# Two transposes of the exponentials ahead of q's maxima in VectorE's queue, with the order settled around them

## The chip, the cores and the metric

The kernel runs on one core of one Trainium2 chip. The metric is the time of one execution on the device in microseconds (us). The kernel before was run three times; the median is taken. One more execution was recorded by the hardware profiler, and all durations and start times below are from that one, counted from its first instruction. The engines are TensorE (PE, with its weight loads as PEld), VectorE (DVE), ScalarE (ACT), GpSimd (POOL) and SyncE (SP), which issues nearly all of the DMA.

## The reference

A transformer-like block with 2048 rows, width 512 and float32 data. Half A is a linear attention with 32 heads of 16 features; half B mixes rows by shifts and then runs an MLP of width 1376. Cut to what is computed:

```python
mod = (silu(c) @ w_mod)                      # six rows of 512: sa, ca, ga, sb, cb, gb
h = layernorm(x) * (1 + ca) + sa
q, k, v = split(h @ wqkv)                    # 32 heads of 16
pq, pk = q @ w_phi, k @ w_phi                # per head, 16x16
phi_q = concat(softmax(pq), softmax(-pq)); phi_k = concat(softmax(pk), softmax(-pk))
kv, z = phi_k^T v, sum over rows of phi_k
o = (phi_q kv) / (phi_q z + 1e-6)
x = x + ga * (o @ wo)
h = layernorm(x) * (1 + cb) + sb             # then half B on h
g = gelu(layernorm(h) @ w1); hs = shifted(g) @ w2; x1 = h + hs
x = x + gb * (x1 + gelu(layernorm(x1) @ w3) @ w4)
```

## The kernel before

Rows are handled in 16 tiles of 128, and mostly in 8 chunks of two tiles (256 rows). Every large product is made of three matmuls on high and low halves in fp32r, so each operand is split by a pair of operations: a copy to the high half on ScalarE (mostly), and a subtraction that gives the low half on VectorE or GpSimd (`hi_lo`, whose subtraction has line 418 on VectorE and 420 on GpSimd in the profile).

The program is a list of 2801 numbered operations, made in one run of the function `body`. Each operation has an engine, the tiles that it reads and writes, and for some of them another engine that could do it. The list is not issued in the order in which it is made: the constant `ORDER` is a permutation of the 2801 numbers, written out by hand. A letter behind a number (V, G or A) puts that operation on VectorE, GpSimd or ScalarE in place of its own engine. `emit` walks `ORDER`, so each engine's queue is the subsequence of `ORDER` that belongs to it, and every engine works through its queue strictly in that order. The constant `SLOT` says for each tile which buffer of its kind it gets. An operation waits by semaphores for the operations whose results it reads, and for the last readers of the buffer that it overwrites.

The first part (to about 145 us) makes k, v and q of all chunks. `q_feat` of tile t (group `q8` for tile 8 and so on) makes q's projection (12 matmuls with 512 columns, PE, `pp<-w,hh`), copies it to `qt` (ScalarE, for most tiles), takes the maximum and the minimum over the 16 features of each head (two reductions on VectorE, L442, `q<-qt` with 512 elements; these are q's maxima), subtracts them (GpSimd, `qe<-qt,q`), takes two exponentials (ScalarE, `qe<-qe`) and stores the result to DRAM.

The sums over k are then turned into two constants: `zbc` (group `z`) and `kvb` (group `kvb`). For `kvb` ScalarE copies the accumulated `kva`, TensorE spreads it by 8 small matmuls (`pp<-const,kvs`), and one VectorE operation masks it into SBUF (`const<-pp,const`, L418, number 682).

From about 145 us on, `phase_a(c)` works on chunk c. `q_phi(c)` loads the stored exponentials of two tiles into `e` (the loads rearrange blocks), sums them per head (`q<-e`, L442), multiplies them by `zbc` (`ez<-e,const`, groups `phi0`, `phi1` and so on) and sums these (`pz<-ez`, L442), then makes the weights of the two tiles in five small operations (group `den0` for the first chunk), scales both `e` by them (`e<-e,q`, GpSimd), and transposes each in blocks of 32 by 32 (`turn`, L762, `pT<-e`; groups `tr0` and `tr1` for the first two tiles). Then TensorE makes the numerators (`num0`: 64 small matmuls `pp<-pT,const`, which read `kvb` and `pT`), the output projection (`o0`: 24 matmuls `pp<-w,oT`), which VectorE adds to x with row sums (L437, `pp<-pp,xl`), then a layer norm (`rs<-mv` on GpSimd is its inverse root), a second one, transposes on TensorE (`pt<-const,n`), the split into `nT` (hi on ScalarE, lo on VectorE), and the first product of half B (`g0`, `pa<-nT,w`, 24 matmuls each half). While the first chunks go through this, the last eight tiles of q are still being made: q8 to q15 lie interleaved with `phi`, `den`, `tr`, `num` and `o` of chunks 0 to 2 in all queues.

From about 204 us on TensorE works through the rest of half A, the shifts and the MLP to the end.

VectorE's queue around the change, by numbers in `ORDER` (the engines' own work between them is left out):

```
708 706 (ez of tiles 1, 0)  709 707 (their sums)  460 459 (q8 max/min)  710-714 (den0)  796 798 (e sums 2, 3)
800 (phi2 sum)  467 (q9)  718 (pT, tile 1)  468 (q9)  590 (q12)  682 (kvb)  716 (pT, tile 0)  802 (phi3 sum)
524 (q10)  803 (den1)  589 (q12)  525 (q10)  722 (oT lo)  ...
```

Of the kernel before, what the change touches and what calls it, by code (L numbers as in the profile page):

```python
# [164 lines left out]
)  # L165
SLOT = {
    "pp": "510234426360573046405216574732325716511600313075732270653365216523706542035040435752736700267672"
          "4243153510404460571",
    "bd": "46",
    "w": "134625cd387165ad28cb09",  # L170
    "rk": "73958dgc",
# [1216 lines left out]
```

## Time and profile before

| what | value |
|---|---|
| runs | 554.64, 554.66, 555.55 us; median 554.66 us |
| profiled execution | 554.69 us; its span from first to last instruction 552.9 us |
| PE busy | 544.9 us (99%) in 4498 matmuls |
| DVE busy | 488.6 us (88%) in 903 instructions |
| ACT busy, POOL busy | 351.7 us (64%), 344.5 us (62%) |
| granted TensorE clock | 0.999 of full speed |
| DMA | 124.90 MB, mean 226 GB/s |

A row of the timeline gives the start in us, the duration in us, the engine, the line of the kernel, the operation, the tiles written and read, the size, and the count when several instructions of one kind follow each other; in brackets stands how long the engine had been idle before, and what released it. Matmuls are pipelined and their ends are modelled, so a row's end can lie a little behind the start of the next. A row of the windows gives, for one stretch of the span, the busy time of each engine and the granted clock.

### The profile page before, as it was taken

How to read it: one execution, taken by the hardware profiler on the slowest of the kernel's cores; microseconds unless marked ns; L12 is line 12 of the kernel's file. 1: busy time of each engine (PE TensorE's matmuls, PEld its weight loads, DVE VectorE, ACT ScalarE, POOL GpSimd, SP SyncE). 2: the span in 40 equal slices, each digit the busy share in tenths (PEclk: the TensorE clock that was granted, in tenths of full speed). 3: DMA queues.
4: the chain of work that ended last, by engine and by line, in shares of the span. 5: the costliest groups of instructions: out<-in, count | busy, mean ns of one | idle time of the engine just before them, and what ended most of it. 6: DMA issues, size and time to landing. Idle time of an engine off the chain costs nothing.

```text
span 552.9 us, 12370 instructions
## 1 busy us (share of the span) xinstructions
PE 544.9 (99%) x4498; PEld 488.1 (88%) x4498; DVE 488.6 (88%) x903; ACT 351.7 (64%) x828; POOL 344.5 (62%) x351
## 2 busy tenths in 40 slices
PE   8999999999989999999999999999999999999997
PEld 7888788878767788888889898999999999999996
DVE  3999999899999999999998878987888868896886
ACT  2899898834436788969888877866434543434540
POOL 2499985979599999978886545234150434254442
PEclk9999999999999999999999999999999999999999
DMA  8982544537736766869987878986689673872022
GB/s 323 392 277 89 175 170 137 176 112 248 205 118 226 249 195 206 275 235 319 292 275 270 242 257 301 339 356 231 284 248 347 245 284 97 264 286 80 25 92 95
DMA packets 63749, 124.90 MB, mean 226 GB/s; under 512 B 7140, under 2 KB 26852, under 8 KB 59592
## 3 DMA queue, kind: packets, MB, share of 16 engines
q1 hardware_dynamic: 63400, 124.04, 66.4%
q8 instruction: 35, 0.57, 0.4%
q14 instruction: 26, 0.21, 0.1%
q10 hardware_dynamic: 288, 0.07, 0.1%
HBM read 89.74 MB, written 34.35 MB: 224 GB/s over the span
## 4 chain that ended last, share of the span: by engine, by line
PE 86%; DVE 7%; POOL 3%; DMA 2%; issue 1%; ACT 0%; DVEq 0%; POOLq 0%
PE pp L471 36%; PE pa L471 27%; PE ac L471 20%; PE pt L480 2%; DVE pz L442 2%; DVE q L442 2%; DMA mod<-in_wmod 1%; PE kva L471 1%; POOL qe L420 1%; DVE pT L762 1%; POOL ez L420 1%; POOL e L420 1%; DVE ez L418 1%; DMA const<-in_c 1%; DVE pp L437 0%
## 5 line engine op out<-in xcount | busy, mean ns | idle before, releaser
L471 PE MATMUL pp<-w,hh 128*128 128x512 f32 x576 | 138.8, 397 | 0.0
L471 PEld LDWEIGHTS pp<-w,hh 128*128 128x128 f32 x576 | 106.7, 188 | 26.1 <-issue 1.6
L471 PE MATMUL pa<-bH,wq 128*128 128x256 f32 x840 | 106.7, 281 | 0.0
L471 PE MATMUL ac<-w,gg 128*128 128x256 f32 x840 | 106.6, 281 | 0.0
L471 PEld LDWEIGHTS ac<-w,gg 128*128 128x128 f32 x840 | 103.4, 189 | 1.1
L471 PEld LDWEIGHTS pa<-bH,wq 128*128 128x128 f32 x840 | 103.1, 189 | 0.9
L471 PE MATMUL pp<-w,sh 128*128 128x512 f32 x192 | 49.4, 399 | 0.0
L471 PE MATMUL pa<-nT,w 128*128 128x256 f32 x384 | 48.3, 282 | 0.8 <-DVE nT L418 0.7
L471 PEld LDWEIGHTS pa<-nT,w 128*128 128x128 f32 x384 | 46.8, 188 | 2.5 <-DVE nT L418 1.2
L471 PE MATMUL pp<-w,oT 128*128 128x512 f32 x192 | 47.4, 395 | 0.0
L471 PEld LDWEIGHTS pp<-w,oT 128*128 128x128 f32 x192 | 35.4, 188 | 8.1 <-DVE oT L418 0.7
L401 ACT ACTIVATE gg<-cu 128x256 fp32r<-128x256 f32 (+1 forms) x56 | 19.1, 359 | 35.1 <-PE ac L471 19.7
L471 PEld LDWEIGHTS pp<-w,sh 128*128 128x128 f32 x192 | 34.6, 188 | 7.5 <-issue 0.8
L588 POOL TENSOR_TENSOR rs<-mv,const 128x2 f32<-128x2 f32 x31 | 23.8, 769 | 25.3 <-ACT mv L595 23.7
L401 ACT ACTIVATE cu<-pa 128x512 f32<-128x512 f32 (+1 forms) x42 | 21.5, 519 | 27.6 <-PE pa L471 22.3
L420 POOL TENSOR_TENSOR gg<-cu,gg 128x128 fp32r<-128x128 f32 (+1 forms) x26 | 15.8, 615 | 33.2 <-ACT gg L401 13.9
L420 POOL TENSOR_TENSOR ez<-e,const 128x1024 f32<-128x1024 f32 x12 | 29.2, 2433 | 5.2 <-DMA dram<-qe 5.1
L401 ACT ACTIVATE gg<-sg 128x512 fp32r<-128x512 f32 x38 | 23.1, 624 | 14.0 <-POOL sg L420 6.0
L420 POOL TENSOR_TENSOR e<-e,q 128x1024 f32<-128x1024 f32 x15 | 28.8, 1938 | 0.4 <-DVE q L418 0.2
L418 DVE TENSOR_TENSOR gg<-cu,gg 128x256 fp32r<-128x256 f32 (+1 forms) x54 | 22.1, 416 | 7.6 <-PE ac L471 4.6
L418 DVE TENSOR_TENSOR gg<-sg,gg 128x512 fp32r<-128x512 f32 x36 | 26.0, 722 | 3.0 <-PE ac L471 1.5
L420 POOL TENSOR_TENSOR ke<-ke,k 128x1024 f32<-128x1024 f32 x14 | 27.2, 1952 | 1.2 <-DVE k L445 1.2
(214 smaller groups left out, 1211.5 us busy)
## 6 DMA issues: line engine op xcount, KB each, us to landing
wq<-dram SPq DMA_DIRECT2D x32, 1024.0 KB, 7.8
dram<-ws SPq DMA_DIRECT2D x35, 256.0 KB, 3.1
xl<-in_x SPq DMA_DIRECT2D x32, 256.0 KB, 4.1
dram<-qe SPq DMA_DIRECT2D x16, 512.0 KB, 3.7
e<-dram SPq DMA_DIRECT2D x64, 128.0 KB, 3.2
raw<-in_w SPq DMA_DIRECT2D x18, 256.0 KB, 3.7
mod<-in_wmod SPq DMA_DIRECT2D x16, 256.0 KB, 5.2
dram<-xl SPq DMA_DIRECT2D x16, 256.0 KB, 3.0
```

Source lines behind the costliest of these rows:

```text
L401: nc.scalar.activation(o(), i(), func, **kw)
L418: dve = ("DVE", 71 + 1.04 * o.n + 90 * (isps(a) and isps(b)), lambda: nc.vector.tensor_tensor(o(), a(), b(), op=op))
L420: pool = ("Pool", cost, lambda: nc.gpsimd.tensor_tensor(o(), a(), b(), op=op))
L442: plan.op("DVE", 65 + 1.04 * a.n + 110 * isps(o), lambda: nc.vector.tensor_reduce(o(), a(), axis=AX.X, op=op), [o], [a])
L471: nc.tensor.matmul(o(), a(), b(), start=s, stop=e, **kw)
L480: nc.tensor.transpose(o(), i(), ident())
L588: plan.op("Pool", 540 + 10 * m, lambda: nc.gpsimd.tensor_tensor(r(), v(), mhalf[:, :m](), op=OP.pow), [r], [v, mhalf])
L762: plan.op("DVE", 71 + 1.04 * o.n, lambda: nc.vector.transpose(o(), i()), [o], [i])
```

## The change

Only `ORDER` and `SLOT` differ. No operation is added, removed or altered. In VectorE's queue the two transposes of the first chunk (718 and 716) come ahead of maxima of q that stood before them: 718 ahead of 467 (q9), 716 ahead of 468 (q9) and 590 (q12). Around them the order is settled anew, which gives, in VectorE's queue of this stretch:

```
708 706 (ez of tiles 1, 0)  709 707 (their sums)  710-714 (den0)  460 459 (q8 max/min)  798 796 (e sums 3, 2)
800 (phi2 sum)  718 (pT, tile 1)  467 (q9)  716 (pT, tile 0)  468 (q9)  590 (q12)  802 (phi3 sum)  682 (kvb)
803 (den1)  589 (q12)  525 (q10)  804 (den1)  524 (q10)  722 (oT lo)  ...
```

So den0 moves ahead of q8's pair, and kvb (682) moves behind pT of tile 0, the rest of q9, q12 and the sum of phi3. In GpSimd's queue the scaling of tile 1 (717) moves ahead of q8's subtraction (461), q11's subtraction (534) moves ahead of the scaling of tile 3 (810), and a split of w3 (1005) ahead of the product of phi5 (909), which still stands ahead of the inverse root of o0 (741). In ScalarE's queue the copy for kvb (680) moves ahead of q9's copy and q8's exponentials, and the second normalised tile of n0 (757) ahead of the first (753). In SyncE's queue the store of q6 moves ahead of a load of x, and a load of the last weights (1481) behind the store of q8. TensorE's queue keeps the same sequence from 129 to 196 us but for one swap of v13 and v14.

Elsewhere in the list operations move by a few places (by 6 on average, counted in `ORDER`, at most 165), 117 of them get another engine (VectorE's queue has 858 operations in place of 871, GpSimd's 358 in place of 347, ScalarE's 736 in place of 734), and buffers are renamed. Seven of these 117 lie in the first 20 us, and all the others behind 290 us. The core of the diff:

```diff
 ORDER = (
...
-    "586 663 293 656 647 294 657 295 683 584 1481 381 684 797 603 685 605 672 383 652 457 708 1033 706 799G 458 "
-    "650 709 707 665 382 460 669G 384 459 903 710 465 862 711 461G 651 712 713 714 796 717G 462 798 654 466 587 "
-    "680 800 463 715G 464 467 718 801G 681 468 588 522 590 682 469G 716 802 905 719 523 720 907G 524 530 721 803 "
...
-    "906 593 594 733 904 687 810G 1001 1482 809 726 1004 1010 534G 734 727 689 735 688 736 812 728 536 694 909G "
...
+    "292 379 583 649 647 293 294 381 295 663 683 584 684 657 797 603 685 672 605 383 652 708 382 384 706 709 457 "
+    "799G 707 458 1033 650 903 669G 710 711 712 713 714 460 465 717G 651 459 798 461G 796 654 800 680 466 715G "
+    "462 718 587 463 464 467 801G 1481 716 681 588 468 522 590 469G 802 905 682 907G 803 589 719 523 720 525 530 "
...
+    "1001 906 593 1004 594 904 534G 733 687 809 726 1010 810G 734 689 727 735 688 536 736 1005G 812 728 694 811 "
+    "909G 737 738 739 729V 740 742 730 535 741 1012 744 813 690G 595 814 1007 743 745 816 537 910 985G 746 747 "
...
 SLOT = {
...
-    "ez": "4988322399990775",
+    "ez": "7388877733881994",
...
-    "pT": "3044399695373795",
+    "pT": "6279733584797084",
...
```

More of the change, by code (lines that the diff above doesn't have):

```diff
@@ L40 @@
 ORDER = (
[124 rows of a table removed]
[124 rows of a table added]
 )
 SLOT = {
[L167 to L171, printed above, removed]
-    "xl": "01lif20gi5bh89hdfh4a36c0kejafg2h50eh36ecj9hl0aac",
-    "st": "03b8g32eh379c16aej5837hgb7h96dj2b",
-    "mv": "14fa06bdj2bdg379c16c68i2h9ie7064a",
-    "rs": "26hc17fi148hj2bdg34j2a19ef1c4f78e",
-    "nm": "57ei9dj54a89cg056afei0548fhi02bd54bd03aiaeg0fj581cg539hi",
@@ L177 @@
-    "xn": "ab75aj6ejag7f54b",
-    "mod": "ekbk73e1dj930hf2ke",
-    "mod2": "1023",
-    "kva": "4",
-    "za": "7",
-    "hh": "0789abe0",
-    "pt": "71713064136760724740255030200105",
-    "raw": "948hcla7b2l2g59fd34940abi351",
-    "k1": "0110502430210140",
-    "ke": "4501639451823940",
-    "k2": "5343025543253140",
-    "vv": "3246ekjhkfh0170l",
-    "qe": "7692282134682731",
-    "q1": "3242123515032015",
-    "qt": "ajj9ib759209",
-    "acc": "clf1e",
-    "kvs": "1",
-    "pz": "1",
@@ L195 @@
-    "q2": "03105351",
-    "e": "5617956458034928",
-    "ez": "4988322399990775",
-    "q3": "1245243214024032",
-    "q5": "44423145",
-    "pT": "3044399695373795",
-    "oT": "4a4ea04b",
-    "nT": "b05444be",
-    "n": "l12l4aaf1h5kje7g",
-    "h": "7519l62c7i1lfkcd",
-    "gf": "21535500",
-    "sh": "92be2cb0",
-    "pa": "720435033552357536277143075740636220453477601263027041460272",
-    "wr": "80061",
-    "ws": "010ie23c3782d1hgibgibgfbd0id69267k7",
-    "gb": "8",
-    "tw": "08935",
@@ L212 @@
-    "bL": "47604149",
-    "nb": "dgdj5dhj4gg4jbjd",
-    "yt": "9fje7gehj940707c",
-    "bH": "23820419431994595628147378657521",
-    "tr": "e10a2k3haldgbhd0",
-    "wq": "e90c934e174e3174e7314e7134e14317e431",
-    "cu": "672egi14hdfl25b7c1364hg9ked6l14g9cd0jblf",
-    "gl": "big235l6",
-    "ac": "26311637061227465013415304762351",
-    "gg": "25789138572584716831287609283795063284107962583265103241806937415809261809713458",
-    "sg": "kf6fka6k0j0k94h3la253c4b4acl7276ki2k97e4",
-    "xb": "9had9ei0fj3haf15",
@@ L224 @@
-    "xc": "5le904k6jhi2fg2i",
-    "uu": "00k2i6ck",
+    "pp": "103254426360573024105642531076565142570060405012650736424542754275304217052353125077021243702025"
+          "7514373375161105643",
+    "bd": "34",
+    "w": "135624cd1803546c28ad79",
+    "rk": "62957dgc",
+    "xl": "01lkf81hf2c3e7faeg28bcia53digl83gf3hbda4h1b335a2",
+    "st": "02c8g25eh2afd3489j672ci3aaif4bh2a",
+    "mv": "13fa04abj5cbh2afd34d47e5ifg9c04f8",
+    "rs": "45hb38fd317ij5cbh21j580f9b3g1jc19",
+    "nm": "76ei9dj61c79ig0648e9g0617eig05ce61adj28e89h0bh67dg3567ie",
@@ new lines @@
+    "xn": "badc2j8ahk60l352",
+    "mod": "ei0k55ae907d1764j8",
+    "mod2": "1023",
+    "kva": "3",
+    "za": "0",
+    "hh": "0789abe7",
+    "pt": "71017321472114171713744334525754",
+    "raw": "3ibhbh069ajk10lf7bk1k7ie2c09",
+    "k1": "0154142304254534",
+    "ke": "4519637451823749",
+    "k2": "1303421130210101",
+    "vv": "dj54b943be4g74hl",
+    "qe": "7602282147569981",
+    "q1": "3202523540132140",
+    "qt": "j6cla90h4cae",
+    "acc": "glib8",
+    "kvs": "j",
+    "pz": "6",
@@ new lines @@
+    "q2": "03105451",
+    "e": "5610345046170836",
+    "ez": "7388877733881994",
+    "q3": "1245243213023042",
+    "q5": "55523450",
+    "pT": "6279733584797084",
+    "oT": "56be67ba",
+    "nT": "a74bbeab",
+    "n": "j9jk0k0f9h050cbf",
+    "h": "4h91j8c4a29jg5a8",
+    "gf": "82474611",
+    "sh": "92ae2da7",
+    "pa": "703114433732744470266315724172066332741566027321035460214535",
+    "wr": "89252",
+    "ws": "gkgi8jd7dfjeh4ge2l1l0e0lbi27d1lla5a",
+    "gb": "6",
+    "tw": "18406",
@@ new lines @@
+    "bL": "93512920",
+    "nb": "7lfdhf3hkffk1e18",
+    "yt": "1ghhfd431lk3j5e0",
+    "bH": "07781924496042747084970213281728",
+    "tr": "49li34c0d4h0f7b7",
+    "wq": "b97d91eb30eb130be310be301beb03b1e30b",
+    "cu": "dj4hfb7kg8id4jl97cg5gfe041h8i7lj02fi8bk7",
+    "gl": "0k0dbcja",
+    "ac": "63050516072335610247706274315620",
+    "gg": "86370698372387960859386014385616354827930168574689574638954160378521943501637285",
+    "sg": "i2i3d253a8a32f8a1d3jbcjlj3gi95g49agk051l",
+    "xb": "9gh1ei25ka3hecd9",
@@ L226 @@
+    "xc": "elee5g38b7k5g7g2",
+    "uu": "0g1d244k",
 }
```

239 rows, old and new, of the table ORDER are left out of this document.

## The prediction

> **What bounds the kernel now.** I read the busy times first, then the windows, to see which stage each engine fills.
>
> ```profile
> PE 544.9 (99%) x4498; PEld 488.1 (88%) x4498; DVE 488.6 (88%) x903; ACT 351.7 (64%) x828; POOL 344.5 (62%) x351
> ```
> ```profile
> 145.00:204.00 59.00, 56.48 (x486) 44.38 (x478) 58.05 (x90) 35.02 (x76) 55.88 (x35) 1.00 0.65 203
> 204.00:549.00 345.00, 345.00 (x2839) 326.49 (x2839) 298.45 (x614) 214.09 (x520) 180.71 (x227) 1.00 0.70 238
> ```
>
> TensorE looks like the only bound, but the windows split that. From 204 to 549 us it is busy 345.00 of 345.00 us, so whatever delay exists at 204 us is carried to the end. From 145 to 204 us, where the change sits, it loses 2.5 us, while VectorE is busy 58.05 and GpSimd 55.88 of 59.00 us: those two pace this stage. The timeline of TensorE shows where it waits.
>
> ```profile
> 157.71 3.04 PE L471 MATMUL pp<-w,hh 128*128 128x512 f32 x12
> 162.47 1.16 PE L471 MATMUL pp<-pT,const 64*32 64x128 f32 x64 [1.72 <-DVE pT L762]
> 163.56 3.03 PE L471 MATMUL pp<-w,hh 128*128 128x512 f32 x12
> 166.43 1.56 PE L471 MATMUL pp<-w,oT 128*128 128x512 f32 x6
> 167.83 2.94 PE L471 MATMUL pp<-w,hh 128*128 128x512 f32 x12
> 170.61 4.32 PE L471 MATMUL pp<-w,oT 128*128 128x512 f32 x18
> ...
> 188.76 0.28 PE L471 MATMUL pa<-nT,w 128*128 128x256 f32 x1
> 189.70 3.03 PE L471 MATMUL pa<-nT,w 128*128 128x256 f32 x23 [0.66 <-DVE nT L418]
> ```
>
> The longest wait, 1.72 us, is that of num0 for the second of the two transposes that are moved. The next is g0's for nT, 0.66 us behind its first matmul. Now VectorE and GpSimd in the same stretch.
>
> ```profile
> 144.80 4.56 DVE L418 TENSOR_TENSOR ez<-e,const 128x1024 f32<-128x1024 f32 x2 [0.23 <-ACT qe L401]
> 149.29 2.48 DVE L442 TENSOR_REDUCE pz<-ez 128x64 f32<-128x1024 f32 x2
> 151.67 1.27 DVE L442 TENSOR_REDUCE q<-qt 128x32 f32<-128x512 f32 x2
> 152.86 0.22 DVE L437 SCALAR_TENSOR_TENSOR pz<-q,pz 128x64 f32<-128x64 f32 x1
> ...
> 154.36 0.29 DVE L418 TENSOR_TENSOR q<-q,pz 128x128 f32<-128x128 f32 x1
> 154.56 2.34 DVE L442 TENSOR_REDUCE q<-e 128x64 f32<-128x1024 f32 x2
> 156.82 1.22 DVE L442 TENSOR_REDUCE pz<-ez 128x64 f32<-128x1024 f32 x1
> 157.94 0.68 DVE L442 TENSOR_REDUCE q<-qt 128x32 f32<-128x512 f32 x1
> 158.54 1.23 DVE L762 STREAM_TRANSPOSE pT<-e 128x1024 f32<-128x1024 f32 x1
> 159.69 1.24 DVE L442 TENSOR_REDUCE q<-qt 128x32 f32<-128x512 f32 x2
> 160.85 0.42 DVE L418 TENSOR_TENSOR const<-pp,const 128x256 f32<-128x256 f32 x1
> 161.18 1.24 DVE L762 STREAM_TRANSPOSE pT<-e 128x1024 f32<-128x1024 f32 x1
> 162.34 1.19 DVE L442 TENSOR_REDUCE pz<-ez 128x64 f32<-128x1024 f32 x1
> ```
> ```profile
> 145.46 2.82 POOL L420 TENSOR_TENSOR ez<-e,const 128x1024 f32<-128x1024 f32 x1 [5.13 <-DMA dram<-qe]
> ...
> 153.09 2.03 POOL L420 TENSOR_TENSOR qe<-qt,q 128x1024 f32<-128x1024 f32 x1 [2.50 <-DVE pz L437]
> 155.08 3.83 POOL L420 TENSOR_TENSOR e<-e,q 128x1024 f32<-128x1024 f32 x2
> 158.87 2.39 POOL L420 TENSOR_TENSOR ez<-e,const 128x1024 f32<-128x1024 f32 x1
> ...
> 175.53 2.40 POOL L420 TENSOR_TENSOR ez<-e,const 128x1024 f32<-128x1024 f32 x1
> 177.89 0.73 POOL L420 TENSOR_TENSOR ws<-wr,ws 128x256 fp32r<-128x256 f32 x1
> 178.59 0.69 POOL L588 TENSOR_TENSOR rs<-mv,const 128x2 f32<-128x2 f32 x1
> ```
>
> Each VectorE row starts where the last one ends, so a position in its queue is a time. The 160.85 row is kvb (682), the two transposes are pT of tile 1 and of tile 0.
>
> **The change part by part.** *VectorE up to num0.* I lay the new sequence on the old durations, from start to start. The sums of ez end at 149.29 + 2.48 = 151.77. den0 follows at once; its five operations take from 152.86 to 154.65, that is 1.8, so they end at 153.6 (before: 154.65). q8's pair (152.86 - 151.67 = 1.2) lasts to 154.7, the two e sums (2.26) to 157.0, the phi2 sum (1.12) to 158.1. pT of tile 1 starts there (before: 158.54). One reduction for q9 (0.6) and pT of tile 0 starts at 159.85 and ends at 161.1. Before it ended at 162.42. So far the change does what its name says: the transpose that num0 waited for is done 1.3 us earlier. Its input has to keep up: GpSimd scales tile 1 from 153.75 (0.15 behind den0, as 153.09 lies behind 152.94), then subtracts for q8 (1.99), then scales tile 0 until 159.6, just ahead of 159.85.
>
> *kvb.* num0 reads kvb as well, and kvb now stands behind pT of tile 0, the other q9 reduction, q12's (1.16 together) and the phi3 sum (1.1). It starts at 163.3 and ends at 163.7; before it ended at 161.27, 1.15 ahead of the transpose. So num0 starts at about 163.8 in place of 162.47: TensorE's q10 ended at 160.75, and its wait grows from 1.72 to 3.0 us. The wait goes from pT to kvb, and **1.3 us are lost at num0** where 1.3 were to be won. The bounds are the transpose alone (161.15, a gain of 1.3) and kvb (163.8); I take kvb, because the matmuls name the tile and nothing lies between. Queued behind num0 on TensorE are q11, o0, q14 in fixed order, and all shift.
>
> *What that costs further on.* TensorE arrives late in a stage that VectorE and GpSimd pace, so the loss counts only where they wait for it.
>
> ```profile
> 175.22 0.69 DVE L437 SCALAR_TENSOR_TENSOR pp<-pp,xl 128x512 f32<-128x512 f32 x1
> ...
> 179.31 0.75 DVE L437 SCALAR_TENSOR_TENSOR h<-pp,rs,const 128x512 f32<-128x512 f32 x1
> ```
>
> Between num0 and this point VectorE has the same work as before in a slightly different order, and every operand is there in time, with one exception: the second addition of o0 started at 175.22, and its matmuls ended at 170.61 + 4.32 = 174.93. The slack was 0.29. With TensorE 1.3 later they end at 176.25, so VectorE, which would be there at some 175.6, waits about 0.7, and the addition comes 1.0 later than before. The layer norm behind it needs the inverse root on GpSimd. There GpSimd too is later: its chain began at 153.75 in place of 153.09, and the phi5 product (175.53) now goes into the buffer of the third transpose, which num1's first half must have read; that half follows num0 by 174.93 - 162.47 = 12.4 on TensorE, so it ends at 163.8 + 12.4 + 0.6 = 176.8. The product then runs from about 176.95 to 179.35 and the inverse root from 179.4 to 180.1, against 178.59 to 179.28. So the 179.31 row moves to 180.15: **0.8 us late**. The two causes run side by side and aren't added. From here to nT and g0 (189.70), and on to g1 at about 204, VectorE and GpSimd have nothing to give (58.05 and 55.88 of 59.00 us), so I carry 0.8 to 204 us and, by the full row behind it, to the end. g0's wait of 0.66 takes up what TensorE is late beyond 0.8. Bounds of this term: 0, if VectorE and GpSimd make up their lateness on operations that wait a little now, and 1.3, if all of num0's loss goes through; 0.8 is what both chains give.
>
> *One collision that stays.* The row of 144.80 holds two products of 1024 elements in 4.56 us, while the sums of the same size take 1.24 each; GpSimd's product, 2.82 long where its like takes 2.39, began at 145.46 in the midst. One VectorE product has waited for GpSimd, by 4.56 - 2 x 1.2 = 2.2 us. The Trainium skill (SBUF — State Buffer, section Who interferes with whom) says that a VectorE instruction with two SBUF inputs and a GpSimd instruction that reads SBUF exclude each other, whoever issues first, and that one with a single SBUF input never contends; this trace agrees, since the transpose of 158.54 ran beside GpSimd's 158.87 in its usual 1.23. The three products stand in the same order after the change, and GpSimd's was released by the store of q5, which is as early or earlier now. If it comes first of the three, the sum of the three is the same. Cost 0; lower bound -2.2, if it came behind both of VectorE's.
>
> *ScalarE, SyncE and the swap in n0.* ScalarE is busy 35.02 of 59.00 us and covers its reordering; the swap of the two normalised tiles makes TensorE's transposes about 0.3 later, which g0's wait of 0.66 covers. The moved loads and stores here (q6's store, a load of last weights behind q8's store) lie tens of us ahead of their readers but for e of tile 5, which is loaded once q8's store has landed, at about 162 as before. Cost 0; without these covers up to 0.3.
>
> *The rest of the order.* Up to 145 us TensorE's sequence differs by exchanges of neighbours, and its inputs are the same. Behind 204 us VectorE has 298.45, GpSimd 180.71 and ScalarE 214.09 of 345.00 us, so the 110 operations that change engines are covered by idle time, one by one. I take 0, with bounds of 0 (nothing is left to win in a row of 345.00) and +1.0, about one exposed operation of GpSimd's size.
>
> **Sum.** 554.69 (the profiled execution, 1.8 us around its span of 552.9) + 0.8 = **555.5 us**. That execution lies 0.03 above the median of 554.66, which I neglect.
>
> **The rivals.**
> *The gain is returned (554.7).* If kvb weren't what num0 waits for, or VectorE absorbed its lateness, num0's 1.3 either way would end at g0, whose lo half of nT stands at the same place in a full queue: the wait moves from num0 to g0, and nothing changes. For it: VectorE at 98% of the stage. Against it: the 0.29 slack at 175.22 and GpSimd's later start.
> *The collision flips (553.3).* GpSimd's product begins at 145.46, and VectorE's second one would have started at 145.95. If q5's store releases GpSimd more than 0.5 us later than before, VectorE runs both products in 2.4 and is 2.2 earlier throughout the stage: 554.69 - 2.2 + 0.8. Against it: in ScalarE's queue q5's exponentials stand no later.
> *More waits behind 204 us (556.5).* The settled order has many new neighbours, and one exposed wait of 1 us adds in full, because TensorE is the bound there.
> *The clock falls (558.5).* If a wait of 3.0 us at num0 let the granted clock drop for the next 12 matmuls, their 3.03 would double and the wait at the o0 addition would grow by 3.0. The row has 1.00 after a wait of 1.72; no run here shows 3.0. The Trainium skill (TensorE: Matmul & The Clock Gate, section What's actually happening) puts the fall behind one idle window of about 3.4 us, which 3.0 doesn't fill; its summary names gaps over some 3 us.
>
> **How the numbers follow.** 0.2% of 554.66 is 1.1 us, about what this measurement can tell from no change: under 553.55 is faster, over 555.77 slower. Forecast 0.50 (555.0 to 556.0; I put 0.36 of it below 555.77 and 0.14 above), gain returned 0.20, collision flips or some other gain 0.12, more waits 0.14, clock 0.04. Faster 0.12, same 0.36 + 0.20 = 0.56, slower 0.14 + 0.14 + 0.04 = 0.32. The range leaves out the faster case, the clock and the top of more waits: 554.2 to 556.7.
>
> **What would show it.** Right: num0's row has an idle time near 3 us that ends on the masking of kvb (L418), not on L762; pT of tile 0 ends near 161.1; the second addition of o0 starts near 176.3 behind an idle VectorE; g1 starts 0.8 later. Wrong: num0 earlier than 162.47; GpSimd's product behind both of VectorE's at 145 us; a TensorE wait behind 204 us.

## The result

The changed kernel took 558.52 us (median), the kernel before beside it 554.90 us. The median counts a disturbed run of 1115.41 us; ratios and intervals leave such runs out here and below, and the other six lie between 556.97 and 559.50 us, with a median of 558.16. The ratio is 1.0059, with a 95% interval of 1.0045 to 1.0073: slower by 3.3 us, where 0.8 had been forecast. The profiled execution took 559.5 us, with a span of 557.4 us and a granted clock of 0.997. By the clock of the whole run, three took 557.79, 558.89 and 559.50 us at 0.997, and three 556.97, 557.58 and 558.52 us at 1.000: 1.0 us apart on average, though the two groups overlap.

### The profile page after: what moved, and what is told of

Same layout as the page of the kernel before. It is cut to its first block, busy times and chain, and to the rows that moved or that the text cites. A ratio compares the mean times of both kernels' runs of the same rounds, so it can differ in the third digit from the quotient of the medians.

```text
span 557.4 us, 12336 instructions
## 1 busy us (share of the span) xinstructions
PE 548.2 (98%) x4498; PEld 489.8 (88%) x4498; DVE 485.3 (87%) x890; ACT 353.7 (63%) x830; POOL 352.0 (63%) x362
## 4 chain that ended last, share of the span: by engine, by line
PE 65%; DVE 8%; POOL 1%; issue 1%; DMA 1%; ACT 0%; DVEq 0%
PE pa L471 27%; PE ac L471 20%; PE pp L471 17%; DVE q L442 2%; DVE pz L442 1%; PE pt L480 1%; DVE ez L418 1%; POOL e L420 1%; DVE pT L762 1%; DMA dram<-qe 1%; POOL ez L420 0%; DVE ke L418 0%; DVE qe L418 0%; DVE k L442 0%; DVE nT L418 0%
## 5 line engine op out<-in xcount | busy, mean ns | idle before, releaser
L471 PE MATMUL pp<-w,hh 128*128 128x512 f32 x576 | 140.6, 401 | 0.0
L471 PEld LDWEIGHTS pp<-w,hh 128*128 128x128 f32 x576 | 107.8, 190 | 27.1 <-issue 1.6
L471 PE MATMUL ac<-w,gg 128*128 128x256 f32 x840 | 106.9, 281 | 0.0
L471 PE MATMUL pa<-bH,wq 128*128 128x256 f32 x840 | 106.8, 282 | 0.0
L471 PEld LDWEIGHTS ac<-w,gg 128*128 128x128 f32 x840 | 103.8, 188 | 1.3
L471 PEld LDWEIGHTS pa<-bH,wq 128*128 128x128 f32 x840 | 103.2, 189 | 0.6
L471 PE MATMUL pp<-w,sh 128*128 128x512 f32 x192 | 49.5, 399 | 0.4 <-DVE nT L418 0.4
L471 PEld LDWEIGHTS pa<-nT,w 128*128 128x128 f32 x384 | 46.9, 188 | 2.4 <-DVE nT L418 1.0
L471 PE MATMUL pa<-nT,w 128*128 128x256 f32 x384 | 48.4, 282 | 0.5 <-DVE nT L418 0.3
L471 PE MATMUL pp<-w,oT 128*128 128x512 f32 x192 | 47.4, 396 | 0.0
L471 PEld LDWEIGHTS pp<-w,oT 128*128 128x128 f32 x192 | 35.5, 188 | 8.1 <-DVE oT L418 0.3
L471 PEld LDWEIGHTS pp<-w,sh 128*128 128x128 f32 x192 | 34.6, 188 | 8.2 <-issue 1.2
L588 POOL TENSOR_TENSOR rs<-mv,const 128x2 f32<-128x2 f32 x31 | 22.2, 715 | 18.9 <-ACT mv L595 15.6
L420 POOL TENSOR_TENSOR sg<-cu 128x128 f32<-128x128 f32 x23 | 14.3, 626 | 29.4 <-ACT cu L401 11.4
L418 DVE TENSOR_TENSOR gg<-sg,gg 128x512 fp32r<-128x512 f32 x37 | 27.9, 755 | 5.2 <-ACT gg L401 3.6
L418 DVE TENSOR_TENSOR gg<-cu,gg 128x256 fp32r<-128x256 f32 (+1 forms) x54 | 21.1, 403 | 9.5 <-PE ac L471 4.2
L420 POOL TENSOR_TENSOR gg<-cu,gg 128x128 fp32r<-128x128 f32 (+1 forms) x26 | 17.7, 688 | 17.9 <-ACT gg L401 5.7
```

The lines of the kernel that those rows point to most:

```text
L418: dve = ("DVE", 71 + 1.04 * o.n + 90 * (isps(a) and isps(b)), lambda: nc.vector.tensor_tensor(o(), a(), b(), op=op))
L420: pool = ("Pool", cost, lambda: nc.gpsimd.tensor_tensor(o(), a(), b(), op=op))
L471: nc.tensor.matmul(o(), a(), b(), start=s, stop=e, **kw)
L588: plan.op("Pool", 540 + 10 * m, lambda: nc.gpsimd.tensor_tensor(r(), v(), mhalf[:, :m](), op=OP.pow), [r], [v, mhalf])
```

## The profile after

The busy times of the page, and windows of the stage and of what is behind it. A window's columns are its length, then PE, PEld, DVE, ACT and POOL busy, the granted clock, DMA share and GB/s.

```profile
PE 548.2 (98%) x4498; PEld 489.8 (88%) x4498; DVE 485.3 (87%) x890; ACT 353.7 (63%) x830; POOL 352.0 (63%) x362
```
```profile
160.00:164.00 4.00, 1.72 (x8) 1.06 (x6) 4.00 (x7) 0.60 (x1) 4.00 (x2) 1.00 0.72 218
164.00:168.00 4.00, 3.87 (x71) 3.05 (x72) 4.00 (x9) 2.12 (x4) 4.00 (x3) 0.71 0.66 185
168.00:172.00 4.00, 4.00 (x17) 3.22 (x16) 2.11 (x6) 2.08 (x5) 3.09 (x3) 0.87 0.46 179
172.00:180.00 8.00, 8.00 (x64) 6.13 (x63) 7.57 (x12) 3.86 (x11) 7.10 (x5) 1.00 0.60 229
...
207.00:553.00 346.00, 345.57 (x2836) 326.55 (x2836) 294.89 (x602) 214.54 (x518) 188.18 (x239) 1.00 0.69 237
```

PE's busy time grew by 3.3 us for the same 4498 matmuls, which a wait can't do: some matmuls became longer. The windows show where about half of it lies. The clock column is below 1.00 from 164 to 172 us and in no other of them, and from 168 to 172 us VectorE, which paces this stage, is idle for 1.9 of 4.00 us. In the kernel before, the clock is 1.00 there (the first row below). Narrower windows of the changed kernel show that the clock was at half, for some 3.4 us, and that the fall began 1.5 us behind the start of num0:

```profile
164.00:168.00 4.00, 4.00 (x19) 3.26 (x18) 3.90 (x9) 2.61 (x6) 4.00 (x3) 1.00 0.93 280
```
```profile
164.10:165.60 1.50, 1.47 (x66) 1.23 (x67) 1.50 (x5) 0.27 (x1) 1.50 (x2) 1.00 0.78 237
165.70:169.00 3.30, 3.30 (x10) 2.51 (x9) 2.96 (x5) 1.75 (x4) 3.30 (x3) 0.50 0.76 237
169.10:172.00 2.90, 2.90 (x14) 2.33 (x14) 1.45 (x4) 2.08 (x5) 1.99 (x2) 1.00 0.22 87
```

The timeline of TensorE names the matmuls:

```profile
158.65 3.07 PE L471 MATMUL pp<-w,hh 128*128 128x512 f32 x12
164.13 1.16 PE L471 MATMUL pp<-pT,const 64*32 64x128 f32 x64 [2.41 <-DVE const L418]
165.22 4.61 PE L471 MATMUL pp<-w,hh 128*128 128x512 f32 x12
...
173.85 4.36 PE L471 MATMUL pp<-w,oT 128*128 128x512 f32 x18
...
323.06 0.94 PE L471 MATMUL pp<-w,sh 128*128 128x512 f32 x3 [0.43 <-DVE nT L418]
```

Read downwards: q10 starts 0.94 later than before (157.71). num0 waits 2.41 instead of 1.72, and the wait ends on kvb's mask (L418), no longer on the transpose (L762). Then q11's 12 matmuls take 4.61 instead of 3.03. The 18 of o0 start 3.24 later (170.61 before). The last row is a wait behind 206 us that the kernel before did not have. VectorE's and GpSimd's timelines, from the two products at 145 us on:

```profile
145.23 4.57 DVE L418 TENSOR_TENSOR ez<-e,const 128x1024 f32<-128x1024 f32 x2
...
160.23 1.23 DVE L762 STREAM_TRANSPOSE pT<-e 128x1024 f32<-128x1024 f32 x1
163.67 0.41 DVE L418 TENSOR_TENSOR const<-pp,const 128x256 f32<-128x256 f32 x1
178.25 0.70 DVE L437 SCALAR_TENSOR_TENSOR pp<-pp,xl 128x512 f32<-128x512 f32 x1 [0.43 <-PE pp L471]
```
```profile
178.96 2.41 POOL L420 TENSOR_TENSOR ez<-e,const 128x1024 f32<-128x1024 f32 x1 [0.90 <-PE pp L471]
181.32 0.70 POOL L588 TENSOR_TENSOR rs<-mv,const 128x2 f32<-128x2 f32 x1
```

The transpose of tile 0 ends at 161.46 (162.42 before), so it is early, and kvb ends at 164.08 (161.27 before). The second addition of o0 waits for TensorE (178.25 against 175.22), and GpSimd's phi5 product waits for num1, as the prediction had it from the changed buffer. VectorE's first product starts 0.43 later than before (145.23 against 144.80), so of TensorE's 0.94 not all has reached the engine that paces the stage. Three places thus show a loss: the start (0.94 at q10), num0 with the slow matmuls behind it, and the order behind 206 us. T1, T2 and T3 below name them as the main cause: T1 the wait at num0 and the clock behind it, T2 the start, T3 the rest.

## The experiments

In the kernels below, a line of the source is often one lower than in the two kernels above (L470 for L471); the operations are the same. Times are medians; each group of kernels has its own runs of the kernel before beside it, given as "before". Where two orders are joined, the first keeps its order up to the cut and the second goes on behind it; such a kernel also has a `SLOT` of its own, so buffers change with the order. The kernels with single moves keep `SLOT`.

### Start, middle and rest by themselves

```diff
 ORDER  (e1_start)
-before: words up to operation 104 (about 20 us)
+changed: words up to operation 104
 before: all others
 ORDER  (e2_middle)
-before: words from there up to operation 858 (about 206 us)
+changed: the same stretch
 ORDER  (e3_rest)
-before: words behind operation 858
+changed: words behind operation 858
```

> The new order up to about 20 us, the old one behind it. T1 (the wait that kvb's mask brings to num0, and the fall of TensorE's clock behind it, make the loss): nothing but the shift of the start, TensorE 0.5 us later from 10 to 20 us and to the end, 555.4 against 554.9 of the kernel before; wait at num0 1.7, q11's 12 matmuls 3.05. T2 (the start is where it is lost, and its shift grows): 556.5 or more. T3 (the rest behind 206 us): as T1.

> The new order from about 20 to 206 us alone (both transposes ahead, kvb's mask behind), the old one before and behind it. T1: wait at num0 2.4 to 3.0 that ends on kvb's mask (L418), the second addition of o0 late; 555.9 in runs where the clock holds and 557.5 where it falls, with q11's 12 matmuls at 4.6 instead of 3.05. T2 and T3: no more than 555.3.

> The old order up to about 206 us, the new one behind it. T1: 554.9 to 555.3. T3 (new neighbours behind 206 us cost a wait that nothing hides): 556.0 to 556.5, with a wait of 0.4 at 321 us that ends on nT (VectorE, L418) and TensorE 1 us later at the end than at 206 us.

Measured, against 554.78 us for before: the start alone 555.94 us, ratio 1.0018 (1.0007 to 1.0029); the middle alone 556.38 us, 1.0025 (1.0016 to 1.0034); the rest alone 556.13 us, 1.0024 (1.0013 to 1.0035). Each of them costs 1 us or more by the ratio, so no theory has it all (the start alone lies between what T1 and T2 expected): 1.0 + 1.4 + 1.3 = 3.7 us, of 3.3 measured for the whole. The wait of 0.4 at 321 us that T3 expected in the rest alone did not come.

The middle tells most. Its 12 runs fall in two groups with nothing between them: 555.49 to 555.89 us at clocks of 0.998 to 1.000 (six runs), 556.86 to 557.21 us at 0.995 to 0.997 (six runs). The gap between the groups' middles is 1.3 us, and the lower group is 0.9 us above before. The profiled run is of the upper group; its timeline of TensorE and its windows show the same fall as the changed kernel:

```profile
158.24 3.06 PE L470 MATMUL pp<-w,hh 128*128 128x512 f32 x12
163.72 1.16 PE L470 MATMUL pp<-pT,const 64*32 64x128 f32 x64 [2.42 <-DVE const L417]
164.81 4.62 PE L470 MATMUL pp<-w,hh 128*128 128x512 f32 x12
```
```profile
164.00:168.00 4.00, 4.00 (x72) 3.12 (x52) 3.97 (x8) 2.12 (x4) 4.00 (x2) 0.61 0.73 205
168.00:172.00 4.00, 4.00 (x18) 3.24 (x17) 2.13 (x5) 2.48 (x6) 3.05 (x3) 0.96 0.32 128
```

### kvb's mask put back ahead, and put behind by itself

In VectorE's queue, by numbers (718 and 716 are the transposes, 682 is kvb's mask):

```diff
 e4_after_kvb_early (from the changed kernel)
-718 467 716 468 590 802 682 803
+718 467 682 716 468 590 802 803
 e5_before_kvb_late (from the kernel before)
-467 718 468 590 682 716 802 524
+467 718 468 590 716 802 682 524
```

> The changed kernel with kvb's mask put back ahead of the transpose of tile 0, so that only the transposes are early. T1: kvb ends by about 161.5 and pT of tile 0 at about 161.9, the wait at num0 falls from 2.4 to 0.5 or less, the clock holds (q11's 12 matmuls 3.05), o0 2 us earlier; 556.0 to 557.0 against 558.5. T2 and T3: the wait goes, the time stays within 0.6 of 558.5, since start and rest are unchanged.

> The kernel before with one move in VectorE's queue: kvb's mask from ahead of the transpose of tile 0 to behind phi3's sum; the transposes stay. T1 (the late mask stretches the wait at num0, and behind a wait of 2.4 us and more TensorE's clock falls in part of the runs): wait at num0 2.6 to 3.0 that ends on the mask, granted clock under 0.9 in the 4 us behind it, q11's 12 matmuls at 4.6; runs in two groups 1.3 apart, about 555.9 and 557.2. Rival (the wait is taken up behind num0, the clock fall belongs to other edits): 554.9 to 555.3, q11 at 3.05.

With the mask early the changed kernel took 557.09 us, just above the range of T1, ratio 1.0036 (1.0024 to 1.0048) to before; all five runs had a clock of 0.999 or 1.000. Against the changed kernel (ratio 1.0059) this is 1.3 us less. The wait at num0 is gone, q11 takes its 3.06 again, and part of what num0 wins is waited for at the next step, o0, which needs VectorE's low half of oT:

```profile
161.29 1.16 PE L470 MATMUL pp<-pT,const 64*32 64x128 f32 x64
162.38 3.06 PE L470 MATMUL pp<-w,hh 128*128 128x512 f32 x12
165.28 0.62 PE L470 MATMUL pp<-w,oT 128*128 128x512 f32 x2
166.42 1.20 PE L470 MATMUL pp<-w,oT 128*128 128x512 f32 x4 [0.52 <-DVE oT L417]
```

With only the mask late, the kernel before took 556.89 us against 554.86, ratio 1.0039 (1.0025 to 1.0054), and all five runs had a clock of 0.996 or 0.997. One operation of 0.4 us, two places further back, costs 2.0 us. The two groups of runs that had been expected are one, the lower clock. The wait is longer than in the changed kernel, and the clock in the window lower:

```profile
163.63 1.16 PE L470 MATMUL pp<-pT,const 64*32 64x128 f32 x64 [2.81 <-DVE const L417]
164.72 4.57 PE L470 MATMUL pp<-w,hh 128*128 128x512 f32 x12
```
```profile
164.00:168.00 4.00, 4.00 (x64) 3.12 (x45) 3.42 (x7) 2.12 (x4) 3.50 (x2) 0.58 0.71 215
```

So the mask's place makes the wait and the fall, without the early transposes and without the rest of the order. The rival, that the wait is taken up behind num0, falls.

### The same wait with TensorE kept at work

```diff
 def phase_a(c):
...
+            if c == 0 and j == 0:
+                fill = ps[0].re("p k c -> p (k c)", (2 * CH,))
+                items = [(fill, wo[0][:, 0, :P], wo[0][:, 0, :], True, True) for _ in range(7)] + items
             marks["num", c] = mms(items, ps, [kvb, pT[j]], hold=[oT], tiles=8)
```

> The changed kernel with TensorE kept at work in the idle time ahead of num0: 7 more matmuls of 128x512 into num0's own PSUM buffer, which num0 overwrites; kvb's mask stays late. T1 (the idle time lets the clock fall): the wait shrinks from 2.4 to 0.7 or less, num0 still starts when the mask is done, q11's 12 matmuls are back at 3.05 and the granted clock at 1.00, no run with a lower mean clock; 557.5 against a median of 558.5. Rival (the clock falls for another reason): runs still fall into two groups, the slower ones with q11 at 4.6; median 558.5.

Measured: 557.13 us (556.97 to 558.02), ratio 1.0044 (1.0030 to 1.0057), and the clock at 1.000 in all five runs, where three of the changed kernel's six had 0.997. By the ratios the changed kernel became 0.8 us faster with seven matmuls more, but the two intervals overlap; the clock and q11's matmuls are the surer sign. The timeline:

```profile
159.55 3.07 PE L471 MATMUL pp<-w,hh 128*128 128x512 f32 x12
162.46 1.78 PE L471 MATMUL pp<-w 128*128 128x512 f32 x7
165.04 1.16 PE L471 MATMUL pp<-pT,const 64*32 64x128 f32 x64 [0.80 <-DVE const L418]
166.12 3.06 PE L471 MATMUL pp<-w,hh 128*128 128x512 f32 x12
```

num0 still waits for the mask, but only 0.80, and q11 takes 3.06. The idle time of TensorE, not the mask's lateness as such and not the amount of work, is what the clock follows here.

This kernel also shows the path behind a late mask while the clock holds. VectorE's rows:

```profile
146.13 1.23 DVE L418 TENSOR_TENSOR ez<-e,const 128x1024 f32<-128x1024 f32 x1
...
177.60 0.70 DVE L437 SCALAR_TENSOR_TENSOR pp<-pp,xl 128x512 f32<-128x512 f32 x1 [0.43 <-PE pp L471]
181.41 0.75 DVE L437 SCALAR_TENSOR_TENSOR h<-pp,rs,const 128x512 f32<-128x512 f32 x1
```

Counted from VectorE's first product at 145 us (144.80 before), num0 starts 1.24 later than before, the second addition of o0 1.05 and the row of h 0.77. The prediction had 1.3, 1.0 and 0.8.

Counted over all kernels, by num0's wait in the kernel's profile: 0 of 62 runs had a mean clock below 0.998 where the wait was at most 0.8 us (seven kernels); 14 of 165 at 1.7 us (the kernel before with 102 of these, and six kernels that keep its middle); 9 of 18 at 2.4 us; 5 of 5 at 2.8 us.

### Only the two transposes early

```diff
 e6_before_two_turns (from the kernel before)
-467 718 468 590 682 716 802
+718 467 682 716 468 590 802
```

> The kernel before with only the two transposes early: pT of tile 1 ahead of the first, kvb's mask and pT of tile 0 ahead of the second maximum of q9. T1: kvb ends near 160.7 and pT of tile 0 near 161.9, the wait at num0 falls from 1.7 to about 1.2 or less, the clock holds, and what num0 wins is given back at the second half of num0's copies and at g0, VectorE having the same work: 554.5 to 555.2, no difference from 554.9. Rival (num0's earlier start goes through): 554.0 or less.

The mask (682) moves forward with them, and stays ahead of the transpose of tile 0. Measured: 555.31 us against 554.86, ratio 1.0009 (1.0000 to 1.0018). num0 starts 1.45 us earlier (161.02 in place of 162.47; 0.27 of it is an earlier q10 in this execution), and all of it is lost on the way. The waits of TensorE in that kernel:

```profile
PE pp L470 <- DVE oT L417: 1.4, 2, 1.3
...
PE pa L470 <- DVE nT L417: 0.7, 1, 0.7
PE pp L470 <- DVE pT L761: 0.5, 1, 0.5
```

num0's wait fell from 1.7 to 0.5, and one of 1.3 for oT stands in its place, at 182.82. VectorE has the same work up to there.

### VectorE's collision at 145 us taken away

```diff
 e9_before_ez_apart (from the kernel before; VectorE, then GpSimd)
-708 706 709 707 460 459 710
+708 709 706 460 459 707 710
-799 669 862 461 717
+799 862 461 669 717
 e13_ez_and_turns: the same, and
-467 718 468 590 682 716 802
+718 467 682 716 468 590 802
```

> The kernel before with the products of phi0 and phi2 kept apart at 145 us: VectorE runs phi1's product, its sum, then phi0's product, so that GpSimd's product of phi2 does not meet it; the product for w7 goes behind q8's on GpSimd. If VectorE is what bounds 145 to 207 us, the product of phi0 takes 1.2 to 1.7 instead of 3.42, den0 starts 0.7 to 1.3 earlier, num0 0.7 earlier, and the time is 554.0 to 554.4. Rival (GpSimd or g0's inputs take it back): 554.7 to 555.0.

> The kernel before with both products kept apart at 145 us, as in the run before, and the two transposes and kvb's mask early. If VectorE's work up to nT is the bound, the transposes add nothing here either: 553.7 to 554.3, the wait at num0 gone, waits at o0 and g0 in its place. If num0 now counts: 553.3 or less.

Measured: 553.87 us against 554.86, ratio 0.9978 (0.9969 to 0.9987); with the transposes early as well 554.29 us against 554.97, 0.9985 (0.9977 to 0.9994). The first is a version that beats both kernels, by 1.0 us over the one before. VectorE's timeline shows phi0's product at 2.17 instead of the 3.4 that it had as the second in the row of 4.56, and den0 at 152.06 instead of 152.86:

```profile
145.14 1.22 DVE L417 TENSOR_TENSOR ez<-e,const 128x1024 f32<-128x1024 f32 x1 [0.23 <-ACT qe L400]
146.40 1.23 DVE L441 TENSOR_REDUCE pz<-ez 128x64 f32<-128x1024 f32 x1
147.54 2.17 DVE L417 TENSOR_TENSOR ez<-e,const 128x1024 f32<-128x1024 f32 x1
...
152.06 0.23 DVE L436 SCALAR_TENSOR_TENSOR pz<-q,pz 128x64 f32<-128x64 f32 x1
```

VectorE 0.8 earlier is worth 1.0 us at the end; num0 1.45 earlier without VectorE is worth nothing. With both (the second kernel) the transposes still add nothing.

### The start's loads and engines, and where the rest loses

```diff
 e10_start_loads (from the kernel before; SyncE)
-35 52 2 42 50 54 56 237 23 31 19 88 27
+52 35 2 42 50 54 56 23 31 19 88 237 27
 e11_start_engines: ORDER of e1_start, with these two moves of SyncE undone
 e12_late_rest: changed order behind about 330 us only
 e14_206_to_330: changed order from about 206 to 330 us only
```

> The kernel before with only the two moves of the start in SyncE's queue: the second part of the modulation's weights ahead of the first rows of x, and the rows xl5 behind four loads of the weights rk. T1 (the start's loss of 1.0 lies in the order of the loads): 555.5 to 556.2, TensorE's waits for the modulation's weights 0.2 to 0.5 longer. T2 (it lies in the operations that change engines): 554.7 to 555.1.

> The new start up to about 20 us with the loads in the old order, the old order behind it: operations change engines and neighbours alone. T1 (loads): 554.7 to 555.2. T2 (engines and neighbours): 555.5 to 556.2, and runs as far apart as with the whole new start (554.6 to 557.3).

> The old order up to about 330 us, the new one from there. If the loss of 1.2 of the rest lies in the waits at g6 and at 321 us: 554.9 to 555.2. If it is spread over the matmuls of the last 220 us: 555.5 to 555.9, TensorE's matmuls pa<-bH,wq of 128x256 at 97.3 or more in all from 330 to 550 us against 97.0, with no wait of its own.

> The new order from about 206 to 330 us alone, the old one before and behind it. The new order behind 206 us cost 1.2, the one behind 330 us nothing. If the loss is made between 206 and 330 us by waits there: 555.8 to 556.2, TensorE 0.8 or more later at 330 us. If it needs both parts: 554.9 to 555.2.

(In the first two of these texts T1 and T2 stand for the start's loads and for its changes of engine.) Measured, against 554.97 us: the loads alone 555.39 us, 1.0008 (0.9999 to 1.0017); the other moves of the start alone 555.61 us, 1.0009 (1.0000 to 1.0018); the order behind 330 us alone 554.95 us, 0.9999 (0.9990 to 1.0008). The order from 206 to 330 us alone, against 555.03: 555.31 us, 1.0006 (0.9998 to 1.0015). The start's two halves share its loss about evenly, and both intervals reach down to 1. The profile of the loads alone has a wait of 0.4 for the weights rk that neither whole kernel has, so that half is not a clean part. A part of the start's loss was made by the cut itself: with the changed start up to 20 us TensorE waits at 29 us for rows that VectorE normalises, which neither whole kernel does (the start alone, then the start without its loads):

```profile
29.25 0.98 PE L479 MATMUL pt<-const,xn 128*128 128x128 f32 x7 [0.56 <-DVE xn L409]
```
```profile
29.62 0.99 PE L479 MATMUL pt<-const,xn 128*128 128x128 f32 x7 [0.66 <-DVE xn L409]
```

The rest's 1.3 us is in neither of its parts: 0.3 and 0.0 by themselves. In the first of these two, the profile has a wait of 0.7 for gf at 325.69; in the rest as a whole TensorE's waits show none behind 206 us, but the matmuls themselves are a little longer. In the window from 330 to 550 us the 840 matmuls of `ac<-w,gg` are busy for 106.9 us in the whole rest and 106.8 in the part behind 330 us, the 768 of `pa<-bH,wq` for 97.3 and 96.9. Before has 106.6 and 97.0. In the whole rest that is 0.6 of the 1.3 us, spread over 1608 matmuls, though most of it in the first group is there in the part behind 330 us too, which costs nothing. Clearer is how long the products `ac<-w,gg` last from the first to the last, in the whole rest and in the part behind 330 us:

```profile
L470 PE MATMUL ac<-w,gg x840: 274/281/312, 351.8 to 550.0; 128*128 128x256 f32 x168
```
```profile
L470 PE MATMUL ac<-w,gg x840: 274/281/320, 351.6 to 549.0; 128*128 128x256 f32 x168
```

The two kernels have the same order there, yet the first takes 0.8 us more, without a wait. So this order does not lose the time by itself; it loses it behind the changed order from 206 to 330 us, or with other buffers. What lengthens the matmuls stays open.

### New up to 140 us, or from there

```diff
 ORDER  (e15_to_140)
-before: words up to operation 646 (about 140 us)
+changed: words up to operation 646
 ORDER  (e16_from_140): the reverse
```

> The new order up to about 140 us, the old one behind it, so that the two orders no longer meet at 20 us, where a wait of 0.6 to 0.7 for xn at 28 us belonged to neither kernel alone. If the start's loss is real: 555.5 to 556.0, TensorE 0.5 to 1.0 later at 146 us. If it was that wait: 554.9 to 555.3.

> The old order up to about 140 us, the new one behind it: the reverse of the run beside it. T1 with additive parts: the changed kernel without its start, 557.3 to 558.0, in two groups 1.3 apart by the clock behind num0. If the start's loss is not real: 558.3 or more.

Measured: 553.78 us against 555.03 for the first, ratio 0.9976 (0.9966 to 0.9987), and 555.75 us, 1.0014 (1.0005 to 1.0024), for its reverse. Both expectations missed. The first is faster than before, because the joint moved GpSimd's product: VectorE's two products come first, and GpSimd waits for them. VectorE's and GpSimd's timelines:

```profile
145.18 2.36 DVE L417 TENSOR_TENSOR ez<-e,const 128x1024 f32<-128x1024 f32 x2 [0.24 <-ACT qe L400]
...
151.04 0.22 DVE L436 SCALAR_TENSOR_TENSOR pz<-q,pz 128x64 f32<-128x64 f32 x1
```
```profile
146.37 3.45 POOL L419 TENSOR_TENSOR ez<-e,const 128x1024 f32<-128x1024 f32 x1 [5.86 <-DMA dram<-qe]
```

GpSimd's release came 0.9 us later than in the kernel before (145.46), the pair takes 2.36 instead of 4.56, and den0 starts 1.8 earlier. The reverse meets a wait of 1.5 us for vv at 145 us, in the joint, that neither kernel has, and its VectorE products are free of GpSimd too; so it cannot be read as the changed kernel without its start. What the start costs can be read from where q10 begins on TensorE. With the changed start it was 158.65 (the changed kernel), 158.09 (mask early), 159.55 (filled) and 158.13 (new up to 140 us), on average 158.6; in the nine profiles with the old start that have no wait of a cut's own 157.44 to 158.24, on average 157.84. That is about 0.8 us, with a scatter as large as itself from run to run. VectorE paces the stage, and its first product at 145 us starts at 145.30 and at 144.88 on average in the same two groups: about 0.4 us of the start reach it, with a scatter of the same size.

## Why the prediction was wrong

**Right: what num0 waits for.** The wait goes from pT to kvb (the 164.13 row names L418), the transpose comes 1.0 earlier (1.3 forecast), and GpSimd's phi5 product waits for num1. Moving the mask alone makes the wait and the fall of the clock, putting it back takes both away.

**Right: the sum of the path when the clock holds.** "0.8 us late" against 0.77 at the same row in the filled kernel, and 0.9 at the end in the middle alone, lower group.

**Mis-sized: the wait itself.** kvb ended at 164.08 instead of 163.7, but TensorE was 0.94 late already, so it waited 2.41 and not 3.0. This is a sign that the start was not free, where the prediction took 0 up to 145 us: 0.4 by VectorE's first product, and 1.0 (0.4 to 1.6) in the start alone, of which a wait of 0.56 belongs to the cut.

**Failed: the clock rival's condition.** It stood at 0.04, since 3.0 us was held to be too short a wait. With a wait of 2.4 us the clock was lower in half of the runs, with 2.81 us in all five. Its place was right (q11), its price was half of what was put: 4.61 against 3.03, 1.6 at the place and 1.3 at the end. All 12 matmuls at half clock would have taken 6.1, but the clock was at half for only some 3.4 us, which costs 1.7. The rival's 558.5 meets the measured median by chance: it lacks the start and the rest, and its price is too high.

**Failed: "The rest of the order", 0 with an upper bound of 1.0.** The order behind 206 us cost 1.3 (0.7 to 1.9). The argument was that idle time on the other engines covers 110 operations one by one. For waits this held nearly: the changed kernel has one of 0.43 at 323 us, and the rest alone none. What the step left out is that matmuls can become longer without a wait. The bounds of the term lay on one side of its value: with TensorE at 345.00 of 345.00 us a new order had little to win and something to lose. TensorE's own sequence is also another one behind 206 us, which the term did not weigh. Which operations do it was not found, and the cause stays open.

Put together: 0.4 from the start (1.0 with the wait of its cut), 0.9 at num0, 1.3 of clock in half of the runs, which is 0.7 on average, and 1.3 from the rest: 3.3 (3.9) against 3.3 measured. That this meets is in part luck, since the parts come from separate runs with intervals of about 0.6 each way.

**Right: the collision.** In the changed kernel it stayed, as forecast (4.57 for the two products). It does flip where GpSimd is released 0.9 later, at the place and by the condition given for the rival. VectorE then gains 1.8 to 2.2, of which 1.2 reach the end: num0's wait, 1.72, all but vanishes, and the rest is TensorE's own work. The Trainium skill (SBUF — State Buffer, section Who interferes with whom) says that whoever issues first holds the shared read path; the trace agrees in both orders, VectorE's product 3.42 when GpSimd came first, GpSimd's 3.45 when VectorE did. The prediction's "never contends" for one SBUF input is wider than that section of the Trainium skill, which excepts VectorE's two-port modes; this case shows it only for transposes (1.23) and sums (1.24).

**"The gain is returned"** was the wrong reading for this change but the right one for its title: the two transposes, with the mask still ahead, gave 1.45 at num0 and nothing at the end.

## What to carry to other kernels

Before moving an operation, list everything behind which its consumer's other operands now stand: here the late operand was a mask of 0.4 us, a few places back, and it cost more than the two moves in the title could win. Where the bounding engine is full, put the bounds of a resettled order on the side of loss: here it was 0.0 and 0.3 us for the two parts of the rest and 1.3 for both. Price a lone wait of TensorE of 2.4 us or more with the slower matmuls behind it.

What shortened this stage was time taken off the engine that paces it. Taking two colliding products apart was worth 1.0 us, starting TensorE 1.45 earlier nothing.

## What the hardware showed that was not expected

The mean clock of the run was below 0.998 in 9 of 18 runs of kernels with one idle time of TensorE of 2.4 us, in 5 of 5 with 2.8 us, in 14 of 165 with 1.7 us, and in none of 62 with 0.8 us or less. Where the fall lies is seen only in the profiled runs, of which three have one behind num0 (waits of 2.41, 2.42 and 2.81). The windows of the changed kernel have 0.50 from 165.7 to 169.0 us and 1.00 on both sides. Half clock for some 3.4 us lowers the mean over 557 us by 0.003, about the distance of the low runs from 1.000. In none of the three did the fall come in the wait itself: it began 1.0 to 1.5 us behind its end, 3.6 to 3.9 us after TensorE had become idle. The Trainium skill (TensorE: Matmul & The Clock Gate, section What's actually happening) calls the window free-running, so that the moment varies; that fits runs that differ at the same wait. Its 3.4 us of idle is longer than the waits that sufficed here, and the measurement decides. Whether num0's small matmuls behind the wait (64*32 in the rows, 1.16 us) count as idle for it was not tried; with them, 2.41 would be 3.57 and 1.72 would be 2.88.

The kernel before had a clock of 0.996 in 8 of 102 runs (555.5 to 556.5 us), and the version with the products apart, whose wait at num0 is 0.6, in none of 11. So a wait of 1.72 may already suffice at times; that the clock of those 8 runs fell at num0 is not shown, since none of them was profiled.
